# Two transformer layers on one core: products with v in three 16-bit passes, one quad later

## The chip, the cores and the metric

The kernel runs on one core of a Trainium2 chip. A core has five engines that run side by side, each through its own instructions in order: PE (TensorE, matrix products; its weight loads are shown apart as PEld), DVE (VectorE), ACT (ScalarE), POOL (GpSimd) and SP (SyncE, which here issues most DMAs). The metric is the device time of one execution in microseconds (us). A difference under 2% is taken as no change.

## The reference

`x` is 2048 rows of 640 numbers. Two layers follow each other, and both use the same weights; a layer is an attention part and an MLP part. The attention has 32 heads of 20 and a sliding window of 256 rows.

```python
def _A_ref(x, wqkv, wo):
    qkv = (x @ wqkv).reshape(B, S, 3, H, Dh) ...          # H = 32, Dh = 20, S = 2048
    scores = jnp.einsum("bhqd,bhkd->bhqk", q, k) * (Dh ** -0.5)
    mask = (idx[:, None] - idx[None, :] >= 0) & (idx[:, None] - idx[None, :] < 256)
    p = _softmax(jnp.where(mask[None, None], scores, -1e9), axis=-1)
    o = jnp.einsum("bhqk,bhkd->bhqd", p, v)
    return o.transpose(0, 2, 1, 3).reshape(B, S, D) @ wo

def _B_ref(x, w1, b1, w2, b2):
    h = jnp.einsum("bsd,df->bsf", x, w1) + b1             # D = 640, F = 1536
    r = jnp.where(h > 0, h, 0)
    return jnp.einsum("bsf,fd->bsd", r * r, w2) + b2

x = x + _A_ref(_layernorm(x), A_wqkv, A_wo)
x = x + _B_ref(_layernorm(x), B_w1, B_b1, B_w2, B_b2)
...                                                       # the same two lines once more
```

## The kernel before

**Units and quads.** The rows are cut into 8 groups of 256; a unit `u` is one group in one layer, 16 in all (`NU`). In a unit the heads go by fours, 8 quads (`NQ`). A query of a unit sees keys of its own unit and of the unit before (`steps_of`: four key blocks of 128, in three steps; units 0 and 8 see only themselves, in two steps).

**Precision.** The large products (`mm3`, line 327, "dense") take every operand as two f16 numbers, a high one and the rest, and do three passes: high by high, high by rest, rest by high. A rest is made by a pair of operations, ACT writes the high half and DVE subtracts. Only the products with v (`pv_quad`, line 838) run in f32, straight from the exp's output.

**One quad** is this chain, with the names that the trace shows:

- M, `max_quad` (line 653): scores of q and k in the bank pair `bb`. DVE merges (666) and reduces (669) them to row maxima, which go through a transposing DMA into two extra rows of the query tile. M runs three quads ahead of S.
- S, `exp_quad` (line 767): the scores once more, less the maxima, into the same pair `bb`. ACT takes the exp (789) into six f32 buffers `pt`, one for each step and half; POOL zeroes what the mask hides (804, 808).
- V, `pv_quad` (line 838): 16 products of `pt` with `vt`, four heads side by side in 32 columns each, the last row of `vt` giving the row sums. ACT copies the result (850), and SP writes it to DRAM.

Since S and M share `bb`, M(n+3) must wait for the exps of S(n), and S(n+1) for the reductions of M(n+3).

**One unit's dense work**, in `stage_` functions that hand out products a few at a time: q, k and values of unit u+1 (`stage_qk`, `stage_v`), the output product of unit u-1 (`stage_o`, from `od`, which `load_o` fetches from DRAM and divides by the row sums), its layernorm and transposing DMA (`y_cross`), and its MLP (`stage_f`: w1, then relu on ACT, square on POOL and the two halves on ACT and DVE, then w2).

**What sets the order.** The program is written out by a small planner: `now` is its clock for PE, `post` and `pump` put work of the other engines at the time at which the planner thinks that it can start, with costs and priorities given by hand, and `together` deals dense products between S, M and V of a unit. Two banks (`mm_tile`) hold all other results of PE. Each engine then runs its instructions in exactly that order, so a wrong guess becomes a wait.

The core of `together` before:

```python
if kind == "v":
    wants += quad[1][0]
work(part, Want(*wants, bank=kind == "v"))
if kind == "s":
    quad = exp_quad(what[1])
...
if kind == "v":
    pv_quad(what[1], quad)
```

so the order is S, dense, M, V, dense, and V belongs to the S just ahead. In units 14 and 15 some dense work is held back (`CARRY`, `KEEP`) for the end, where the last V's result has to go through DRAM.

## Time and profile before

| what | value |
|---|---|
| median of 2 runs (lowest to highest) | 1580.69 us (1580.55 to 1580.83) |
| the execution that was profiled | 1585.88 us |
| its span, first to last instruction | 1584.2 us |
| busy share of PE, DVE, ACT, POOL | 98%, 59%, 46%, 38% |
| PE without work over the whole span | 29 us |
| of that, before 230 us | 23 us |
| a unit in the middle of a layer | 96.6 us |

The span is read from the page's first line, the idle time of PE from 1584.2 - 1555.0. Durations below come from this one execution; the median of the runs is 3.5 us below its span. A group's line in the profile shows the line of the code, the engine, the operation, what is written and read, the number of instructions, the time in which at least one ran, and the mean of one. The lines on which the argument rests are shown in the prediction.

### The profile page before, as it was taken

What the parts mean: (1) busy time and instruction counts of PE and PEld (TensorE: products, weight loads), DVE (VectorE), ACT (ScalarE), POOL (GpSimd) and SP (SyncE); (2) the same over time, 40 slices, a digit from 0 to 9 for tenths busy, and PEclk for the clock granted to TensorE, in tenths of its full rate; (3) what the DMA queues carried; (4) which work ended last, traced back from release to release, by engine and by line L of the source; (5) the groups of instructions that cost most, each with busy time, mean ns of one, the idle gap of its engine ahead of it and who ended that gap; (6) DMA issues with size and microseconds to landing.
All of it is one profiled execution on the core that took longest, in us unless ns stands there. A gap on an engine that the chain in (4) does not pass through costs nothing.

```text
span 1584.2 us, 51151 instructions
## 1 busy us (share of the span) xinstructions
PE 1555.0 (98%) x21570; PEld 1167.1 (74%) x21570; DVE 928.6 (59%) x1910; ACT 733.5 (46%) x1593; POOL 607.9 (38%) x1291
## 2 busy tenths in 40 slices
PE   8888999999999999999999999999999999999999
PEld 7665778777777777777777777777777777777777
DVE  8776664565655566465465646566465565556542
ACT  4454545345354444534434454444534445445522
POOL 1232535335343352534414253343524435344522
PEclk9999999999999999999999999999999999999999
DMA  9764343352534625345253533525344253441120
GB/s 270 192 175 125 69 116 83 98 115 65 121 80 108 122 50 123 87 106 108 62 138 81 117 91 107 111 54 120 86 120 94 67 132 68 123 90 58 30 65 19
DMA packets 243341, 160.35 MB, mean 101 GB/s; under 512 B 91176, under 2 KB 226856, under 8 KB 243112
## 3 DMA queue, kind: packets, MB, share of 16 engines
q1 hardware_dynamic: 236744, 147.58, 38.6%
q10 hardware_dynamic: 6368, 9.50, 2.0%
q8 instruction: 169, 2.77, 0.8%
q14 instruction: 60, 0.49, 0.1%
HBM read 84.68 MB, written 52.95 MB: 87 GB/s over the span
## 4 chain that ended last, share of the span: by engine, by line
PE 93%; DVE 2%; DMA 2%; ACT 1%; issue 1%; POOL 0%; SPq 0%; ACTq 0%; DVEq 0%; POOLq 0%
PE acc L327 72%; PE pv L838 11%; PE bb L653 5%; PE bb L767 5%; ACT pt L789 1%; DMA x<-in_A_x_dram 1%; PE bb L775 0%; DMA qt<-mT 0%; DVE mx L669 0%; PE bb L678 0%; DVE bb L633 0%; DMA o<-ot 0%; DVE bst L353 0%; DMA xt<-in_A_x_dram 0%; DVE bb L666 0%
## 5 line engine op out<-in xcount | busy, mean ns | idle before, releaser
L789 ACT ACTIVATE pt<-bb 128x512 f32<-128x512 f32 (+1 forms) x736 | 374.0, 600 | 226.0 <-PE bb L767 198.8
L804 POOL TENSOR_SCALAR_AFFINE_SELECT pt<-pt 128x256 f32<-128x256 f32 x448 | 187.2, 420 | 539.7 <-ACT pt L789 525.6
L327 PE MATMUL acc<-y,w_s 128*128 128x256 f16 x2880 | 328.3, 273 | 0.1
L327 PE MATMUL acc<-w_s,hh 128*128 128x320 f16 (+1 forms) x2340 | 326.8, 298 | 0.0
L327 PEld LDWEIGHTS <-w_s 128*128 128x128 f16 x2880 | 276.5, 98 | 51.3 <-issue 15.0
L327 PEld LDWEIGHTS <-hh 128*128 128x128 f16 x2340 | 221.9, 98 | 97.6 <-issue 12.7
L669 DVE TENSOR_REDUCE mx<-bb 128x4 f32<-128x1024 f32 x224 | 273.9, 1223 | 6.6
L327 PEld LDWEIGHTS <-wq_s 128*128 128x128 f16 x2400 | 230.1, 98 | 46.8 <-issue 14.0
L327 PE MATMUL acc<-yT,wq_s 128*128 128x256 f16 x2250 | 258.8, 273 | 2.3 <-DVE qd L510 0.9
L808 POOL TENSOR_SCALAR_AFFINE_SELECT pt<-pt 128x256 f32<-128x256 f32 x512 | 223.1, 458 | 92.3 <-ACT pt L789 91.0
L1023 DVE TENSOR_TENSOR hh<-r,hh 128x256 f16<-128x256 f32 x192 | 94.6, 516 | 225.1 <-ACT hh L1020 218.2
L838 PE MATMUL pv<-pt,vt 128*32 128x128 f32 (+1 forms) x3840 | 189.5, 330 | 0.2 <-POOL pt L804 0.2
L850 ACT COPY ot<-pv 128x256 f32<-128x256 f32 x128 | 47.6, 372 | 286.2 <-PE pv L838 286.2
L1017 POOL TENSOR_TENSOR r<-r 128x256 f32<-128x256 f32 x192 | 114.2, 616 | 157.9 <-ACT r L1013 155.9
L666 DVE COPY_PREDICATED bb<-maskq,bb 128x256 f32<-128x256 uint16 x224 | 93.3, 423 | 98.6 <-PE bb L653 96.8
L327 PE MATMUL acc<-wo_s,od 128*128 128x320 f16 x960 | 140.5, 302 | 3.4 <-DVE od L924 1.9
L838 PEld LDWEIGHTS pv<-pt,vt 128*32 128x32 f32 x3840 | 104.8, 109 | 40.1 <-POOL pt L808 5.5
L327 PE MATMUL acc<-wq_s,yT 128*128 128x320 f16 x900 | 130.6, 300 | 1.4 <-DVE y L378 0.9
L327 PEld LDWEIGHTS <-od 128*128 128x128 f16 x960 | 91.8, 98 | 48.6 <-issue 6.4
L1013 ACT ACTIVATE r<-acc,b1s 128x256 f32<-128x256 f32 x192 | 80.5, 471 | 85.8 <-PE acc L327 84.7
L327 PEld LDWEIGHTS <-yT 128*128 128x128 f16 x900 | 85.5, 98 | 40.7 <-issue 7.8
L364 POOL TENSOR_TENSOR bmv<-bmv,neghalf 128x1 f32<-128x1 f32 x64 | 45.2, 712 | 156.0 <-DVE bmv L358 155.5
(96 smaller groups left out, 1241.6 us busy)
## 6 DMA issues: line engine op xcount, KB each, us to landing
qt<-qk SPq DMA_DIRECT2D x30, 480.0 KB
kt<-qk SPq DMA_DIRECT2D x30, 480.0 KB
qk<-qd SPq DMA_DIRECT2D x17, 640.0 KB
o<-ot SPq DMA_DIRECT2D x256, 42.0 KB
od<-o SPq DMA_DIRECT2D x14, 640.0 KB
qk<-yl SPq DMA_DIRECT2D x13, 640.0 KB
qk<-qd SPq DMA_DIRECT2D x17, 320.0 KB
xt<-in_A_x_dram SPq DMA_DIRECT2D x16, 320.0 KB
```

The source lines that it names most:

```text
L327: nc.tensor.matmul(acc, lhs(a, c), rhs(b, c), start=(k == 0), stop=(k == 3 * nk - 1))
L653: nc.tensor.matmul(flat[e][rows, o:o + b - a], qt[r, p, i * P + 64 * h:i * P + 64 * (h + 1)], kt[r, p, a + to:b + to], start=True, stop=Tr ...
L666: nc.vector.copy_predicated(wins[:, :, 4 * Q:], later, wins[:, :, :Q])
L669: nc.vector.tensor_reduce(most, wins[:, :, Q:], axis=mybir.AxisListType.X, op=ALU.max)
L767: nc.tensor.matmul(bb[e][rows, k, o + a:o + b], kt[r, 2 * qd + j, ko + 64 * h:ko + 64 * (h + 1)], qt[r, 2 * qd + j, q0 * P + a:q0 * P + b] ...
L789: nc.scalar.activation(box["pt"][:, :o], bb[e][:, k, :o], AF.Exp, scale=SCALE / (QS * QS))
L804: nc.gpsimd.affine_select(out=m, in_=m, pattern=[[0, 2], [-1, P]], compare_op=ALU.is_gt, fill=0.0, base=0, channel_multiplier=1)
L808: nc.gpsimd.affine_select(out=m, in_=m, pattern=[[0, 2], [1, P]], compare_op=ALU.is_ge, fill=0.0, base=0, channel_multiplier=-1)
L838: nc.tensor.matmul(pv[32 * jj:32 * (jj + 1), q0 * P:(q0 + qn) * P], vf[:, c:c + 32], pj[:, j, :], start=(k == 0), stop=(k == len(steps) - ...
L1013: nc.scalar.activation(box["r"], acc[:, f, :], AF.Relu, bias=b1s[:, f0 + f:f0 + f + 1], scale=1.0 / (YS * WS))
L1017: nc.gpsimd.tensor_tensor(box["r"], box["r"], box["r"], op=ALU.mult)
L1023: nc.vector.tensor_sub(hh[:, 1, f, :], box["r"], hh[:, 0, f, :])
```

## The change

It does four things.

1. From unit 2 on (`WHOLE = 2`), the values are stored as two f16 halves in the same bytes, and a probability is read as two 16-bit numbers out of one f32 word: its upper 16 bits as bf16 (`hi`), and an f16 rest that is written over its lower 16 bits (`lo`). The products with v run three passes: hi by high, lo by high, hi by rest. The exp gets a bias (`lift`, a factor of 2^10). The rests are new subtractions (`low` in `exp_quad`): per quad of three steps six of 512 columns, four on DVE and two on POOL (all on DVE in the last six quads). `stage_v` gets a subtraction on DVE too. A product of f32 was two records in the profile; a product of 16 bits is one, with a weight load of its own.
2. `pv_quad` of a quad no longer follows its own S: it is held in `behind` and put right after the S of the next quad (`beside`), or after an M where the planner finds it ready.
3. `load_o` is cut in two: `fetch_o` starts the load from DRAM as soon as the last `pv_quad` of a unit is put, into a ring `r` that the MLP uses for its relu (five buffers in place of four), and `load_o` does the division.
4. `stage_v` is no longer at a fixed place among the dense work: a new `Pair` hands out its products when the other dense work has to wait.

Some priorities change (0.8 and 0.9 in place of 1 or 2), and `flow` waits for all masks of a quad in place of the first step's.

```diff
+WHOLE = 2
...
+    def values(u, i):
+        raw = vts[(2 * u + i) % 6]
+        if u < WHOLE:
+            vf = raw.unsqueeze(1)
+        else:
+            vf = raw.bitcast(F16).rearrange("p (a n) -> p a n", a=2)
+        return vf, vf[:, :, :H * (DH + 1)].rearrange("p a (h d) -> p a h d", d=DH + 1)
...
+    class Pair:
...
+        def go(self):
+            c = None if self.mid else self.first.go()
+            if c is None:
+                c = self.fill.go()
+                self.mid = c is not None
+                if c is None:
+                    c = self.first.go()
+            return c
...
 def stage_v(u, which=range(4)):
+        if u > 2:
+            yield Want(unread[u - 2], bank=False)
...
+                def low(hd=hd, src=src):
+                    nc.vector.scalar_tensor_tensor(hd[:, 1], src, s, hd[:, 0], op0=ALU.mult, op1=ALU.subtract)
...
-    def exp_quad(n):
+    def exp_quad(n, beside=None):
...
+        if beside is not None:
+            pv_quad(*beside)
...
-                    nc.scalar.activation(box["pt"][:, :o], bb[e][:, k, :o], AF.Exp, scale=SCALE / (QS * QS))
+                    halves = box["pt"].rearrange("p (n a) -> p n a", a=1)
+                    box["lo"] = halves.bitcast(F16)[:, :, 0]
+                    box["hi"] = halves.bitcast(BF16)[:, :, 1]
+                    nc.scalar.activation(box["pt"][:, :o], bb[e][:, k, :o], AF.Exp, bias=lift, scale=SCALE / (QS * QS))
...
+                    on, eng, each = nc.vector, "D", 1.1
+                    if 2 * k + e in (3, 5) and n < NQ * NU - 6:
+                        on, eng, each = nc.gpsimd, "G", 1.95
+
+                    def low(a=a, b=b, box=box, on=on):
+                        on.tensor_tensor(box["lo"][:, a:b], box["pt"][:, a:b], box["hi"][:, a:b], op=ALU.subtract)
...
+                passes = (("hi", 0), ("lo", 0), ("hi", 1)) if uv >= WHOLE else (("pt", 0),)
+                for m, (b, a) in enumerate(passes):
...
+                                nc.tensor.matmul(pv[32 * jj:32 * (jj + 1), q0 * P:(q0 + qn) * P],
+                                                 vf[:, a, c:c + 32], pj[:, j, :], start=(k == 0 and m == 0),
+                                                 stop=(k == len(steps) - 1 and m == len(passes) - 1),
+                                                 skip_group_check=True, tile_position=(0, 32 * jj))
...
+        if qd == NQ - 1:
+            unread[u].end = now[0]
+            fetch_o(u, u >= NU - 2)
...
+    def fetch_o(u, late=False):
+
+        need(*hjs.pop(u - 1, ()))
...
+            val = sb.tile([P, KC, T], F32, name="ov", tag="r", bufs=1)
...
             if kind == "s":
-                quad = exp_quad(what[1])
+                behind.append((what[1], exp_quad(what[1], behind.pop() if values else None)))
...
-            parts += [stage_qk(u + 1, (0,)), stage_v(u + 1, range(2)), stage_o(u - 1), lambda: (y_cross(u - 1), iter(()))[1], stage_qk(u + 1, (1,)), stage_v(u + 1, range(2, 4))]
+            parts += [stage_qk(u + 1, (0,)), stage_o(u - 1), lambda: (y_cross(u - 1), iter(()))[1], stage_qk(u + 1, (1,))]
+            fill = stage_v(u + 1)
```

**How PE's order changes.** Counted from the two instruction orders, with the number of dense products between the groups (qkv is `stage_qk` and `stage_v`, o is `stage_o`). Before, units 3 to 13 are all alike; now each unit differs, and units 4 to 7 come again as 10 to 13 with small changes. A `|` stands ahead of each S.

```
units 3 to 13 before:
| S qkv50 M V qkv25 | S qkv30 o15 M V o30 | S o15 qkv25 M V qkv40 | S qkv37 M V qkv3 w1 35
| S w1 45 M V w1 35 | S w1 45 M V w1 20 w2 16 | S w2 36 M V w2 28 | S w2 36 M V w2 28
unit 2 now:
| S qkv45 M V qkv82 | S qkv3 o27 M o33 qkv50 | S V qkv25 M w1 15 | S V w1 30 M w1 45
| S V w1 25 M w1 45 | S V w1 20 w2 4 M w2 32 | S V w2 20 M w2 36 | S V w2 24 M w2 4 V w2 24
unit 10 now:
| S V qkv30 M qkv38 | S V qkv22 o15 M o45 qkv75 | S V w1 15 M w1 35 | S V w1 35 M w1 45
| S V w1 35 M w1 15 w2 20 | S V w2 24 M w2 28 | S V w2 24 M w2 32 | S V w2 16 M qkv25
unit 11 now:
| S V qkv35 M qkv45 | S V qkv30 M o60 qkv50 | S V qkv25 M w1 20 | S V w1 35 M w1 45
| S V w1 35 M w1 40 | S V w1 5 w2 24 M w2 36 | S V w2 24 M w2 32 | S V w2 24 M w2 4 qkv10
unit 12 now:
| S V qkv40 M qkv40 | S V qkv30 M qkv15 o42 | S V o18 qkv5 M qkv70 | S V w1 30 M w1 40
| S V w1 35 M w1 40 | S V w1 35 M w2 44 | S V w2 24 M w2 32 | S V w2 24 M w2 12 V w2 8 qkv5
unit 13 now:
| S qkv45 M qkv85 o15 | S V o23 M o22 qkv75 | S V M w1 40 | S V w1 35 M w1 45
| S V w1 30 M w1 30 w2 8 | S V w2 24 M w2 32 | S V w2 24 M w2 32 | S V w2 24 M qkv45
unit 15 and the end, before:
| S w2 24 M V w2 16 | S w2 28 M V w2 4 o23 | S o22 M V o15 w2 4 | S w2 24 M V w2 8 tr8
| S tr2 w1 25 M V w1 20 | S w1 40 V w1 25 | S w1 40 V | S w1 30 V w2 108 o60 w2 16 tr5 w2 12 tr5 w2 8 w1 180 w2 180
unit 15 and the end, now (unit 14 ends with M V):
| S M o45 | S V o15 tr5 M tr5 w1 25 | S V w1 35 M w1 60 | S V w1 30 M w1 30 w2 20
| S V w2 24 M w2 40 | S V w2 40 V | S w2 20 V | S V o60 tr10 w1 180 w2 180
```

Three of these places word for word. The end on PE; `vt` are values, `hh` with `w_s` is w2 of unit 14, `od` with `wo_s` the output product of unit 15. Before:

```order
L838 MATMUL pv<-pt,vt_93 32x256 x4
L838 MATMUL pv<-pt,vt_92 32x128 x4
L838 MATMUL pv<-pt,vt_89 32x128 x4
L838 MATMUL pv<-pt,vt_88 32x256 x4
L327 LDWEIGHTS hh
L327 MATMUL acc<-w_s,hh 128x320
```

and now:

```order
L912 LDWEIGHTS vt_90
L912 MATMUL pv<-pt,vt_90 32x256
L912 LDWEIGHTS vt_90
L912 MATMUL pv<-pt,vt_90 32x256
L363 LDWEIGHTS od
L363 MATMUL acc<-wo_s,od 128x320
```

The 108 products of w2 that stood between the last V and the output product have moved ahead of it.

Unit 13, third quad, on PE, ahead of M (L653 before, L706 now; `kt` and `qt` are keys and queries). Before, products of `stage_qk` stand there:

```order
L327 MATMUL acc<-yT,wq_s 128x256
L327 LDWEIGHTS wq_s
L327 MATMUL acc<-yT,wq_s 128x256
L653 LDWEIGHTS qt
L653 MATMUL bb_133<-kt_85,qt 64x256
```

and now V of the second quad:

```order
L912 LDWEIGHTS vt_92
L912 MATMUL pv<-pt,vt_92 32x256
L706 LDWEIGHTS qt
L706 MATMUL bb_135<-kt_87,qt 64x256
L706 LDWEIGHTS qt
L706 MATMUL bb_136<-kt_87,qt 64x256
```

V has moved from behind M to between S and M, and 25 products of q, k or values have moved ahead of S.

On DVE, around the merge (COPY_PREDICATED) and the reduction of M while w1 goes over to w2; `hh` is the MLP's rest. Before:

```order
L1023 TENSOR_TENSOR hh<-r,hh 128x256 x6
L666 COPY_PREDICATED bb_133<-maskq,bb_133 128x4x64
L669 TENSOR_REDUCE mx<-bb_133 128x4
L666 COPY_PREDICATED bb_134<-maskq,bb_134 128x4x64
L669 TENSOR_REDUCE mx<-bb_134 128x4
L1023 TENSOR_TENSOR hh<-r,hh 128x256 x2
```

and now (in a quad of unit 8, whose own key block has 256 columns):

```order
L1112 TENSOR_TENSOR hh<-r,hh 128x256 x2
L880 TENSOR_TENSOR pt<-pt 128x512 x2
L880 TENSOR_TENSOR pt<-pt 128x256
L1112 TENSOR_TENSOR hh<-r,hh 128x256 x2
L719 COPY_PREDICATED bb_135<-maskq,bb_135 128x4x64
L722 TENSOR_REDUCE mx<-bb_135 128x4
L719 COPY_PREDICATED bb_136<-maskq,bb_136 128x4x64
L722 TENSOR_REDUCE mx<-bb_136 128x4
L1112 TENSOR_TENSOR hh<-r,hh 128x256 x2
```

The subtractions `pt<-pt` have come between the MLP's work and the merge.

More of the change, by code (lines that the diff above doesn't have):

```diff
@@ L1112, in portion, with together @@
             yield c
-    def together(ns, ms, dense, cost, share=1.0, whole=True, after=None, pace=0):
+    def together(ns, ms, dense, cost, share=1.0, whole=True, after=None, pace=0, flush=False, fill=()):
         ts = list(turns(ns, ms, pace))
@@ L1118, in together @@
         done = part = 0.0
-        quad = None
-        s = Stream(dense)
+        s = Pair(dense, iter(fill))
         def work(part, w):
@@ L1144, in together @@
                 wants += [trips[m // NQ, j, m % NQ] for j in range(2)]
-            if kind == "v":
-                wants += quad[1][0]
-            work(part, Want(*wants, bank=kind == "v"))
+            values = kind == "s" and bool(behind)
+            if values:
+                wants += [j for ms in behind[0][1][1] for j in ms]
+            if kind is None and m is None and behind:
+                work(part, Want(*(j for ms in behind[0][1][1] for j in ms)))
+                pv_quad(*behind.pop())
+            work(part, Want(*wants, bank=values))
             if kind == "s":
-                quad = exp_quad(what[1])
+                behind.append((what[1], exp_quad(what[1], behind.pop() if values else None)))
                 for it in late:
@@ L1270 @@
         share = 1.0 - KEEP / cost if last else 1.0 - CARRY / cost if u == NU - 2 else 1.0
-        together(quads, ahead, dense, cost, share, u < NU - 2, after=(lambda: load_o(u - 1, last)) if u > 1 else None, pace=NQ)
+        if last:
+            load_o(u - 1, True)
+        together(quads, ahead, dense, cost, share, u < NU - 2, after=(lambda: load_o(u - 1)) if 1 < u < NU - 1 else None, pace=NQ, flush=u >= NU - 2, fill=fill)
     load_o(NU - 1, True)
```

175 lines of the change are left out of this document (110 added, 65 removed).

## The prediction

> **What bounds the kernel now.** I read the page first, then busy time by stretches, then one quad (four heads of one unit) in order of time, then the end. The page:
>
> ```profile
> span 1584.2 us, 51151 instructions
> PE 1555.0 (98%) x21570; PEld 1167.1 (74%) x21570; DVE 928.6 (59%) x1910; ACT 733.5 (46%) x1593; POOL 607.9 (38%) x1291
> PE 93%; DVE 2%; DMA 2%; ACT 1%; issue 1%; POOL 0%; SPq 0%; ACTq 0%; DVEq 0%; POOLq 0%
> ```
>
> PE is the chain. By stretches (span, then PE, PEld, DVE, ACT and POOL busy with counts, granted clock, DMA share, GB/s):
>
> ```profile
> 124.00:136.00 12.00, 7.33 (x65) 4.15 (x63) 5.58 (x14) 4.40 (x8) 3.58 (x9) 0.72 0.59 158
> 230.00:1380.00 1150.00, 1149.99 (x16376) 865.28 (x16366) 671.44 (x1321) 532.52 (x1160) 456.09 (x976) 1.00 0.42 98
> 1380.00:1512.00 132.00, 128.88 (x2030) 95.55 (x2033) 71.43 (x134) 71.44 (x159) 67.53 (x146) 1.00 0.25 61
> 1512.00:1584.00 72.00, 69.15 (x598) 54.55 (x586) 23.44 (x53) 14.62 (x36) 13.42 (x21) 1.00 0.15 46
> ```
>
> From 230 to 1380 us PE does not stop once: 1149.99 of 1150. So there the time is PE's work, every us taken off it is a us gained, and any new wait of PE is a us lost in full. One quad there, by order of time (start, duration):
>
> ```profile
> 1046.75 0.75 PE L767 MATMUL bb<-qt,kt 62*64 62x192 f16 x32
> 1047.44 5.06 PE L327 MATMUL acc<-w_s,hh 128*128 128x320 f16 x36
> 1047.55 3.05 ACT L789 ACTIVATE pt<-bb 128x512 f32<-128x512 f32 x6 [0.68 <-PE bb L767]
> ...
> 1050.32 1.12 POOL L808 TENSOR_SCALAR_AFFINE_SELECT pt<-pt 128x256 f32<-128x256 f32 x3
> ...
> 1052.43 0.76 PE L653 MATMUL bb<-kt,qt 60*64 60x256 f16 x38
> ...
> 1053.12 1.51 PE L838 MATMUL pv<-pt,vt 128*32 128x256 f32 x32
> 1053.30 0.43 DVE L666 COPY_PREDICATED bb<-maskq,bb 128x256 f32<-128x256 uint16 x1
> ...
> 1054.56 3.98 PE L327 MATMUL acc<-w_s,hh 128*128 128x320 f16 x28
> ...
> 1055.36 1.23 DVE L669 TENSOR_REDUCE mx<-bb 128x4 f32<-128x1024 f32 x1
> ...
> 1058.46 0.75 PE L767 MATMUL bb<-qt,kt 62*64 62x192 f16 x32
> ```
>
> I call L767 S (scores), L653 M (row maxima of a later quad), L838 V (products with v), L327 dense. S and M share the bank pair bb, so each waits for the other's reader: M for the exps of S, which end 3.85 us after S starts (1047.55 + 3.05 - 1046.75); S for the reductions of M, which end 4.16 us after M starts (1055.36 + 1.23 - 1052.43). Here M comes 5.68 us after S and S 6.03 us after M: 1.8 and 1.9 us to spare. That spare time is why PE never waits.
>
> **The change, part by part.**
>
> *V in halves.* V takes 1054.56 - 1053.12 = 1.44 us. Dense takes (1052.43 - 1047.44) / 36 = 0.139 us for 320 columns, 0.433 ns a column. A quad's V is 16 products, two blocks of 256 and two of 128 columns for four heads that run side by side: 768 columns a pass. f32 as four passes is 4 x 0.333 = 1.33, which leaves 0.11 us to fill and drain. Three f16 passes: 1.00 + 0.11 = 1.11 us, 0.33 less. Units 3 to 7 and 9 to 15 have 96 such quads; unit 8 has eight of half the work and unit 2 eight with half the blocks in halves: 104 quads' worth, **-34 us**. Bounds: the passes at exactly 3/4 of 1.44 give -37. On the other side stand the weight loads, now 48 a quad instead of 32:
>
> ```profile
> 1004.27 1.03 PEld L838 LDWEIGHTS pv<-pt,vt 128*32 128x32 f32 x32
> ```
>
> At their 0.032 us each they would need 1.54 us: +10. S and M issue 32 and 38 f16 products in 0.69 us (1047.44 - 1046.75, 1053.12 - 1052.43), 0.018 to 0.022 us each, and 48 of those need 0.87 to 1.04 us, so I take -34. The Trainium skill ("TensorE: Matmul & The Clock Gate", section "Wait — 56ns, not 53.3ns?") says that starts never come closer than about 25 ns; by it V would be 48 x 25 ns + 0.11 = 1.31 us and the gain an estimated 14 us. M's 38 in 0.69 us disagree with it.
>
> *V behind S.* The exps write six buffers, and V of the quad before, which reads them, now stands right behind S. The first exp therefore waits for V's first third as well, about 0.37 us: M's earliest place becomes S + 4.2. S's stays M + 4.2.
>
> *The order of PE.* The front part lists the dense products between the groups. Short places, with 0.113 us for a product of 256 columns and 0.139 for one of 320: unit 2 has M to S with 15 products of 256, 2.3 of 4.2 us needed (-1.9). In the same way: unit 4, 0.75; unit 5, 2.3 in three places; unit 6, 1.9; unit 7, 2.9, most of it where V stands directly before M (1.8 of 4.2 us); unit 10, 0.75; unit 11, 2.3; unit 12, 1.9; unit 13, 2.4; unit 14, 0.75; unit 15, 6.0 (S comes after M and V alone, and then M follows S with nothing between). Sum **+24 us**, where the row of 230 to 1380 had 0.01. The dense products that stood there are not lost: they ran earlier, where od or y2 was waited for, values first.
>
> *The end.* Today's rows:
>
> ```profile
> 1507.21 0.75 PE L767 MATMUL bb<-qt,kt 62*64 62x192 f16 x32
> ...
> 1507.89 3.45 PE L327 MATMUL acc<-y,w_s 128*128 128x256 f16 x30
> ...
> 1511.01 1.12 POOL L808 TENSOR_SCALAR_AFFINE_SELECT pt<-pt 128x256 f32<-128x256 f32 x3
> 1511.27 1.55 PE L838 MATMUL pv<-pt,vt 128*32 128x256 f32 x32
> ...
> 1512.75 14.84 PE L327 MATMUL acc<-w_s,hh 128*128 128x320 f16 x108
> ...
> 1527.43 8.31 PE L327 MATMUL acc<-wo_s,od 128*128 128x320 f16 x60
> ...
> 1535.58 2.34 PE L327 MATMUL acc<-w_s,hh 128*128 128x320 f16 x16
> ...
> 1541.57 6.62 PE L327 MATMUL acc<-y,w_s 128*128 128x256 f16 x58
> ```
>
> The last V's way through DRAM to od (1512.75 to 1527.43, 14.7 us) lies under 108 products of unit 14; the layernorm (1535.58 to 1541.57, 6.0 us) under 36 more. In the new order V is followed at once by the 60 of od, and these by the transposes: unit 14's products are all gone. So PE waits some 13 us there (14.7, less what the adds of those products held DVE up) and 4.7 before w1. The last S has no dense product before its V: the last mask ends 4.92 us after S (1511.01 + 1.12 - 1507.21), the last subtraction (0.66, below) at 5.6, and V would be due at 1.8: 4.2 with its last passes; the quad before, with 20 products, 1.4. Sum **+23 us**; the bounds are 12 (od ready sooner) and 28.
>
> *Clock.* The longest wait of PE today costs more than itself:
>
> ```profile
> PE tr L731 <- DVE x L949: 3.4, 1, 3.4
> ```
>
> Behind it the clock granted over 124 to 136 us is 0.72, which is 3.4 us of 12. Waits of 13 and 4 us at the end, and those of unit 15, may each bring one to three of these: **+5** (0 to 9). Today's own waits after 1380 (3.1 of 132, a part at the same layernorm and od) go: **-2**.
>
> *The new subtractions.* Per full quad six of 512 columns, four on DVE and two on POOL, and four on DVE for a unit's values. The nearest rows:
>
> ```profile
> L1023 DVE TENSOR_TENSOR hh<-r,hh x192: 361/426/860, 159.7 to 1563.7; 128x256 f16<-128x256 f32 x192
> L444 DVE TENSOR_TENSOR yl<-xt,yl x52: 814/817/834, 190.8 to 1399.5; 128x640 f16<-128x640 f32 x52
> L1017 POOL TENSOR_TENSOR r<-r x192: 605/612/1149, 158.5 to 1562.7; 128x256 f32<-128x256 f32 x192
> ```
>
> Between 256 and 640 columns DVE's 512 come to 0.66 us (361 to 817 ns); the order has 420: +277 us, plus 56 for the values at about 0.43: DVE goes from 928.6 to some 1230 us, 77%. POOL's 188 at twice 612 ns add 230: 838 us, 53%. Both stand off PE's path as long as the spare 1.8 us hold, and by the lists above only some 0.8 are left. L1023 shows 361 ns at best and 860 at worst, L1017 605 and 1149: the two engines hold each other up when both read SBUF. For delays of PE from this I take **+12 us**, one for each unit with halves; bounds 0 and 65 (second rival).
>
> *Nothing:* the exp's bias, values at another scale, value rows in the ring (off PE, and the waits for od are counted above).
>
> **Sum.** 1584.2 - 34 + 24 + 23 + 5 - 2 + 12 = 1612 us of span. The execution profiled took 1585.88; the median of the runs, 1580.69, is 3.5 us below its span. I take off 4 to 5: **1607 us, +1.7%**.
>
> **Rivals.**
> 1. *The waits are covered* (faster). M may start before the last exp, and a later quad may catch up. Price: without the 24, 23, 5 and 12, 1584.2 - 36 - 3.5 = 1545 us; with half of them 1577. Against it: no product stands in those places. It decides if PE's busy share stays at 98%.
> 2. *DVE and POOL become the bound* (slower). In the w1 stretch a quad has 11.2 us (5.6 + 5.6 in the new order). If SBUF reads of the two exclude each other, 8 masks at 0.37, 5.3 squares (80 dense products, 15 to each) at 0.61 and 2 subtractions at 1.22 on POOL make 8.6, four at 0.66 and 5.3 at 0.36 on DVE 4.5: 13.1. At three such quads in 12 units that is up to 65 us in place of 12: 1660; with half, 1635. It decides from about 0.5 us a quad. For it: the pairs of ends above. Against: the rows hold some start-up that need not exclude. The Trainium skill ("SBUF — State Buffer", section "Who interferes with whom") states this as a rule: a VectorE operation with two inputs in SBUF and a GpSimd one that reads SBUF lock each other out for the whole instruction.
> 3. *The halves do not run at pace* (no gain in V). If weights or operands four bytes apart slow the passes to today's 1.44 us: 1607 + 34 = 1641.
>
> **Chances.** Forecast 0.42 (1585 to 1612), rival 1 0.17 (0.07 of it below 1549), rival 2 0.33, rival 3 0.08. Two per cent, about what a measurement of this kernel can tell from no change, are 1549 and 1612 us. Faster 0.07; within 0.42 + 0.10 = 0.52; slower 0.33 + 0.08 = 0.41. The range leaves out the lower half of rival 1 and the far end of rival 2: 1576 to 1645; the forecast's own is 1585 to 1612.
>
> **What would show it.** V: groups of 1.1 us on PE. Order: waits of PE on ACT's pt and DVE's mx of 1 to 3 us, once a unit, and none before. End: one PE gap of over 10 us in front of the od products, and a granted clock below 1 behind it. Subtractions: DVE near 77%, POOL near 53%, and POOL's masks longer than 406 ns where rival 2 holds. I am wrong if PE's idle time stays under 40 us (rival 1) or if waits on DVE and POOL sum to more than 60 (rival 2).

## The result, and the profile after

The changed kernel takes 1762.57 us (median of 2 runs, 1761.62 to 1763.53) against 1580.69: the ratio is 1.115, with a 95% interval from 1.110 to 1.120. It is 182 us slower. The profiled execution took 1761.62 us, its span is 1759.9.

From the page of the changed kernel: the span, the busy times, and the shares of the chain that ended last.

```profile
span 1759.9 us, 55219 instructions
...
PE 1591.2 (90%) x23234; PEld 1203.9 (68%) x23234; DVE 1323.7 (75%) x2417; ACT 799.5 (45%) x1593; POOL 954.2 (54%) x1495
...
PE 33%; DVE 24%; POOL 15%; ACT 13%; issue 11%; DMA 3%; SPq 1%; POOLq 0%; ACTq 0%; DVEq 0%
```

V's products (count, busy us, mean ns), before and after:

```profile
L838 PE MATMUL pv<-pt,vt 128*32 128x128 f32 (+1 forms) x3840 | 189.5, 330 | 0.2 <-POOL pt L804 0.2
L912 PE MATMUL pv<-pt,vt 128*32 128x128 bf16 (+5 forms) x5504 | 164.0, 261 | 12.4 <-DVE pt L880 4.0
```

PE is idle for 168.7 us (1759.9 - 1591.2) where it was idle for 29.2, and it is busy for 36 us longer, although V's own busy time fell by 25.5. PE was 93% of the chain; now DVE, POOL and ACT together have more of it than PE. No engine but PE is above 75%, so this isn't an engine that ran out of time.

The waits of PE in the changed kernel (sum, times, longest, in us):

```profile
PE bb L820 <- DVE mx L722: 66.3, 76, 1.8
PE bb L706 <- ACT pt L848: 24.9, 44, 3.1
PE acc L363 <- ACT od L1007: 18.2, 3, 10.5
PE tr L784 <- DVE x L1035: 6.0, 1, 6.0
```

L820 is S, L706 is M, L363 dense, and L912 V. S waits for the reductions of M (L722), and M for the exps of S (L848): both waits are on the bank pair `bb`. The stretches that the prediction looked at, and the end (span, then PE, PEld, DVE, ACT and POOL busy with counts, granted clock, DMA share, GB/s):

```profile
230.00:1380.00 1150.00, 1065.74 (x16119) 811.38 (x16117) 907.36 (x1588) 528.48 (x1054) 692.97 (x1057) 0.99 0.37 89
1570.00:1690.00 120.00, 85.28 (x1332) 60.17 (x1330) 80.85 (x125) 47.74 (x96) 59.99 (x96) 0.87 0.11 33
1690.00:1760.00 70.00, 55.09 (x430) 42.45 (x430) 20.40 (x47) 13.18 (x32) 12.15 (x18) 0.86 0.11 36
```

In the first, PE was idle for 0.01 us before and is for 84 now. One quad there, in order of time (start, duration, in brackets the idle time ahead of it and what ended that):

```profile
1088.61 0.27 PE L820 MATMUL bb<-qt,kt 62*64 62x192 f16 x1
...
1089.25 0.75 PE L820 MATMUL bb<-qt,kt 62*64 62x192 f16 x31 [0.38 <-DVE mx L722]
...
1089.93 1.23 PE L912 MATMUL pv<-pt,vt 128*32 128x256 bf16 x48
...
1090.56 0.69 ACT L848 ACTIVATE pt<-bb,lift 128x512 f32<-128x512 f32 x1 [1.09 <-PE pv L912]
...
1091.09 4.00 PE L363 MATMUL acc<-y,w_s 128*128 128x256 f16 x35
...
1093.37 1.87 ACT L848 ACTIVATE pt<-bb,lift 128x512 f32<-128x512 f32 x3
1093.42 1.15 DVE L880 TENSOR_TENSOR pt<-pt 128x512 f16<-128x512 f32 x1 [0.26 <-POOL pt L863]
...
1095.02 1.03 PE L706 MATMUL bb<-kt,qt 60*64 60x256 f16 x38
...
1095.76 0.92 DVE L880 TENSOR_TENSOR pt<-pt 128x512 f16<-128x512 f32 x1 [1.19 <-POOL pt L867]
...
1095.97 5.08 PE L363 MATMUL acc<-y,w_s 128*128 128x256 f16 x45
1096.04 1.78 POOL L867 TENSOR_SCALAR_AFFINE_SELECT pt<-pt 128x256 f32<-128x256 f32 x3
1096.59 0.61 DVE L1112 TENSOR_TENSOR hh<-r,hh 128x256 f16<-128x256 f32 x1
...
1097.49 0.91 DVE L880 TENSOR_TENSOR pt<-pt 128x512 f16<-128x512 f32 x1 [0.30 <-POOL pt L867]
1097.79 1.48 POOL L880 TENSOR_TENSOR pt<-pt 128x512 f16<-128x512 f32 x1
1098.30 1.25 DVE L1112 TENSOR_TENSOR hh<-r,hh 128x256 f16<-128x256 f32 x1
...
1099.47 0.41 DVE L719 COPY_PREDICATED bb<-maskq,bb 128x256 f32<-128x256 uint16 x1
...
1101.20 0.24 PE L820 MATMUL bb<-qt,kt 62*64 62x192 f16 x1
...
1101.52 1.22 DVE L722 TENSOR_REDUCE mx<-bb 128x4 f32<-128x1024 f32 x1
...
1102.79 0.75 PE L820 MATMUL bb<-qt,kt 62*64 62x192 f16 x31 [1.35 <-DVE mx L722]
```

Read it as a loop. The exps of S end at 1095.24, 6.6 us after the first product of S (before: 3.85). That product is alone: it uses the first bank of the pair, and the other 31 wait until the maxima of the second bank are reduced. M starts at 1095.02, but DVE touches its result only at 1099.47. Four operations stand ahead in DVE's queue: two subtractions, which wait for POOL's masks (1.19 and 0.30 us), and two rests of the MLP (L1112). The second of these takes 1.25 us, beside a subtraction on POOL; over the whole run L1112 has a median of 0.42 us with nothing on POOL beside it and of 0.63 with something. The last reduction ends at 1102.74, 7.7 us after M (before: 4.16), and the rest of the next S has waited for it for 1.35 us. V itself does what was predicted: 48 products in 1.16 us (1089.93 to 1091.09).

The end, rows of the same kernel:

```profile
1686.23 0.62 PE L912 MATMUL pv<-pt,vt 128*32 128x256 f16 x7 [0.23 <-DVE pt L880]
...
1694.18 0.96 DVE L1000 RECIPROCAL rs<-rs 128x64 f32<-128x64 f32 x2 [8.00 <-DMA rs<-o]
...
1697.40 11.33 PE L363 MATMUL acc<-wo_s,od 128*128 128x320 f16 x60 [10.55 <-ACT od L1007]
...
1712.62 0.76 PE L427 MATMUL bb<-ident,xt 128*128 128x128 f32 x5 [3.35 <-DVE xt L402]
```

The last V's way through DRAM leaves PE idle for 10.55 us, and the 60 products behind it take 11.33 us in place of 8.31; the granted clock of the stretch is 0.86.

### The profile page after: what moved, and what is told of

Read it like the earlier page. It is cut to its first block, busy times and chain, and to the rows that moved or that the text cites. A ratio compares the mean times of both kernels' runs of the same rounds, so it can differ in the third digit from the quotient of the medians.

```text
span 1759.9 us, 55219 instructions
## 1 busy us (share of the span) xinstructions
PE 1591.2 (90%) x23234; PEld 1203.9 (68%) x23234; DVE 1323.7 (75%) x2417; ACT 799.5 (45%) x1593; POOL 954.2 (54%) x1495
## 3 DMA queue, kind: packets, MB, share of 16 engines
q1 hardware_dynamic: 236744, 147.58, 33.5%
## 4 chain that ended last, share of the span: by engine, by line
PE 33%; DVE 24%; POOL 15%; ACT 13%; issue 11%; DMA 3%; SPq 1%; POOLq 0%; ACTq 0%; DVEq 0%
PE acc L363 23%; ACT pt L848 10%; DVE mx L722 7%; POOL pt L867 6%; DVE pt L880 5%; PE pv L912 4%; POOL pt L863 4%; PE bb L820 3%; DVE hh L1112 2%; POOL pt L880 2%; DVE bb L719 2%; POOL r L1106 1%; PE bb L706 1%; POOL bmv L400 1%; ACT r L1102 1%
## 5 line engine op out<-in xcount | busy, mean ns | idle before, releaser
L848 ACT ACTIVATE pt<-bb,lift 128x512 f32<-128x512 f32 x736 | 450.8, 691 | 293.8 <-PE pv L912 241.5
L880 DVE TENSOR_TENSOR pt<-pt 128x512 f16<-128x512 f32 (+1 forms) x436 | 378.5, 879 | 237.6 <-POOL pt L863 141.1
L863 POOL TENSOR_SCALAR_AFFINE_SELECT pt<-pt 128x256 f32<-128x256 f32 x448 | 225.0, 505 | 488.6 <-ACT pt L848 458.8
L363 PE MATMUL acc<-y,w_s 128*128 128x256 f16 x2880 | 340.3, 278 | 2.2 <-DVE y L414 1.2
L363 PE MATMUL acc<-w_s,hh 128*128 128x320 f16 (+1 forms) x2340 | 331.4, 298 | 3.7 <-DVE hh L1112 3.7
L363 PEld LDWEIGHTS <-w_s 128*128 128x128 f16 x2880 | 280.6, 100 | 54.1 <-issue 13.0
L867 POOL TENSOR_SCALAR_AFFINE_SELECT pt<-pt 128x256 f32<-128x256 f32 x512 | 272.6, 554 | 78.4 <-ACT pt L848 78.4
L363 PEld LDWEIGHTS <-hh 128*128 128x128 f16 x2340 | 221.2, 98 | 99.7 <-issue 9.9
L722 DVE TENSOR_REDUCE mx<-bb 128x4 f32<-128x1024 f32 x224 | 272.2, 1221 | 5.2
L363 PE MATMUL acc<-yT,wq_s 128*128 128x256 f16 x2250 | 258.3, 273 | 4.9 <-DVE yl L546 1.5
L363 PEld LDWEIGHTS <-wq_s 128*128 128x128 f16 x2400 | 230.9, 98 | 42.4 <-issue 9.3
L880 POOL TENSOR_TENSOR pt<-pt 128x512 f16<-128x512 f32 (+1 forms) x204 | 247.8, 1232 | 1.3
L912 PE MATMUL pv<-pt,vt 128*32 128x128 bf16 (+5 forms) x5504 | 164.0, 261 | 12.4 <-DVE pt L880 4.0
L1112 DVE TENSOR_TENSOR hh<-r,hh 128x256 f16<-128x256 f32 x192 | 124.2, 674 | 52.3 <-ACT hh L1109 50.3
L820 PE MATMUL bb<-qt,kt 62*64 62x64 f16 (+3 forms) x3552 | 101.1, 234 | 68.9 <-DVE mx L722 66.3
L363 PE MATMUL acc<-wo_s,od 128*128 128x320 f16 x960 | 143.1, 307 | 21.3 <-ACT od L1007 18.2
L1106 POOL TENSOR_TENSOR r<-r 128x256 f32<-128x256 f32 x192 | 131.6, 705 | 34.9 <-ACT r L1102 34.6
L820 PEld LDWEIGHTS <-kt 62*64 62x64 f16 x3552 | 70.2, 108 | 103.8 <-issue 98.1
L363 PEld LDWEIGHTS <-od 128*128 128x128 f16 x960 | 94.0, 100 | 66.2 <-ACT od L1007 19.4
L706 PE MATMUL bb<-kt,qt 60*64 60x64 f16 (+3 forms) x4256 | 107.4, 224 | 25.7 <-ACT pt L848 24.9
L363 PE MATMUL acc<-wq_s,yT 128*128 128x320 f16 x900 | 128.2, 299 | 0.5 <-DVE kt L414 0.5
```

The lines of the kernel that those rows point to most:

```text
L363: nc.tensor.matmul(acc, lhs(a, c), rhs(b, c), start=(k == 0), stop=(k == 3 * nk - 1))
L706: nc.tensor.matmul(flat[e][rows, o:o + b - a], qt[r, p, i * P + 64 * h:i * P + 64 * (h + 1)], kt[r, p, a + to:b + to], start=True, stop=Tr ...
L722: nc.vector.tensor_reduce(most, wins[:, :, Q:], axis=mybir.AxisListType.X, op=ALU.max)
L820: nc.tensor.matmul(bb[e][rows, k, o + a:o + b], kt[r, 2 * qd + j, ko + 64 * h:ko + 64 * (h + 1)], qt[r, 2 * qd + j, q0 * P + a:q0 * P + b] ...
L848: nc.scalar.activation(box["pt"][:, :o], bb[e][:, k, :o], AF.Exp, bias=lift, scale=SCALE / (QS * QS))
L863: nc.gpsimd.affine_select(out=m, in_=m, pattern=[[0, 2], [-1, P]], compare_op=ALU.is_gt, fill=0.0, base=0, channel_multiplier=1)
```

## The experiments

All are single executions with a profile; the kernel before, run beside them, took 1581.2 to 1582.1 us. The planner decides PE's order anew whenever a product, a dependency or a price that it knows of changes. In runs 1, 3 and 8 to 11 it wrote PE's order of the changed kernel, product for product. In runs 2, 5, 6, 7 and 12 to 15 it wrote another, so these compare the order too; run 4 starts from the kernel before. "A" in the first expectations is the theory that the subtractions cost the time, "B" that the order does.

**1. No subtractions.**

```diff
 def low(a=a, b=b, box=box, on=on):
-    on.tensor_tensor(box["lo"][:, a:b], box["pt"][:, a:b], box["hi"][:, a:b], op=ALU.subtract)
+    pass
...
-pj = box[b][:, part]
+pj = box["hi" if b == "lo" else b][:, part]
```

> The changed kernel with every instruction in its order but the 640 subtractions that make the rests of the probabilities (436 on DVE, 204 on POOL): they are left out, and the pass that would read a rest reads the upper half again. Theory A (the subtractions, by the time they take and by blocking on DVE and POOL, push the reductions, exps and masks back, and PE waits for those): most of the 182 us go, 1595 to 1640 us. Theory B (the order itself, V between S and the exps and the short places between the groups, makes the waits): 1700 us or more.

Measured 1642.4, just above the range of theory A: the subtractions of the probabilities cost 120 us, and some 60 are left. PE's order is the same, and DVE's too but for the subtractions.

**2. Values whole**, the rest of the change kept: `WHOLE = 16` in place of 2.

> All values and probabilities stay whole (f32 products with v, no subtractions), and the rest of the change stays: V one quad later, value rows in the ring, values filling waits; the order is planned anew for it. Theory A: 1580 to 1610 us. Theory B: 1650 us or more, since V still stands between S and the exps.

Measured 1644.2: 62 us of loss in a kernel without any halves. It is not run 1 with whole values, though. With f32 products the planner puts V right behind M in 83 of the 128 quads and right behind S in 42; in the changed kernel it is 21 and 102. That the two times agree doesn't show what V's passes are worth.

**3. Exp without bias.** `bias=lift` taken out of the exp, everything else as changed.

> The changed kernel with the exp's bias left out (the factor 2^10 on the probabilities is missing, nothing else differs). In the changed kernel one exp takes 696 ns at the median against 605 before. If the bias makes that, exps return to about 605 ns and, with six of them in each quad's chain, the time falls by 30 to 60 us; if the exp is longer for another reason (the four-byte words it writes are read by others at the time), both stay.

Measured 1747.5, 15 us less, half of the least that was expected. Run 4 takes the bias by itself; runs 1 and 8, and 2 and 5, differ by it alone.

**4. The kernel before, with a bias in its exp.**

```diff
-nc.scalar.activation(box["pt"][:, :o], bb[e][:, k, :o], AF.Exp, scale=SCALE / (QS * QS))
+nc.scalar.activation(box["pt"][:, :o], bb[e][:, k, :o], AF.Exp, bias=lift, scale=SCALE / (QS * QS))
```

> The kernel before, with a bias operand (zero) in the exp and nothing else. The prediction priced the bias at nothing. If its 90 ns an exp fit into the 1.8 us that M has to spare: 1580 to 1587. If they do not: 1595 or more, with waits of PE on ACT's pt.

Measured 1597.3, 16 us more. The groups of the exp (count, busy, mean ns), first of the kernel before, then of this one:

```profile
L789 ACT ACTIVATE pt<-bb 128x512 f32<-128x512 f32 (+1 forms) x736 | 374.0, 600 | 226.0 <-PE bb L767 198.8
```

```profile
L791 ACT ACTIVATE pt<-bb,lift 128x512 f32<-128x512 f32 (+1 forms) x736 | 440.6, 687 | 222.4 <-PE bb L769 193.2
```

One operand that is read from SBUF makes each exp 87 ns longer. The stretch from 230 to 1380 us of this kernel shows that it reaches PE without a wait to be seen:

```profile
230.00:1380.00 1150.00, 1149.72 (x16257) 860.77 (x16254) 663.38 (x1309) 573.62 (x1152) 446.00 (x970) 1.00 0.40 97
```

PE is as busy as before at the same clock, but gets through 16257 products in place of 16376. Over the whole run it is idle for 29.0 us, as before (29.2), and busy for 1566.6 us in place of 1555.0 with the same products. Stalls too short to be counted as idle would do that; that they are what the profile counts as busy is argued, not shown. The Trainium skill ("ScalarE: Activation LUTs", section "What ACT_TABLE_LOAD costs") says that an operand of one number per partition adds about 93 ns to an ACTIVATE; the traces agree with their 87.

**5. Values whole and no bias** (runs 2 and 3 together).

> Values whole, no subtractions, no bias, V one quad later: the order alone. The kernel with the bias took 1644. If the order makes those 62 us: 1630 to 1640. If the exps, 90 ns longer each by the bias, make them: 1585 to 1610.

Measured 1612.5: the order that the planner writes for whole values, that of run 2, costs 31 us, and the bias on top of it 32 (1644.2). From the first S of the last unit to the end of the span it takes 153.7 us (1457.1 to 1610.8), where the kernel before took 139.7 (1444.5 to 1584.2). That is 14 of the 31; a unit in mid-run takes 97.3 in place of 96.6, and unit 14 takes 7 more.

**6. V at its own quad**, with the halves, the subtractions and the bias.

```diff
-yield 1 - share, None, m
+yield 1 - share, ("v", n), m
...
-behind.append((what[1], exp_quad(what[1], behind.pop() if values else None)))
+quad = exp_quad(what[1])
...
+if kind == "v":
+    pv_quad(what[1], quad)
```

> The changed kernel with V back at its own quad: M, then V of the quad whose scores were just taken, as before the change. Halves, subtractions, the bias, the filling and the ring stay. Theory 1 (V one quad later is the dear part of the order: standing right behind S it delays every exp and so every M): most of the 60 us that were left without subtractions come back, 1690 to 1725. Theory 2 (the delay is what hides the subtractions; without it PE waits for them ahead of every V): 1780 or more, with waits of PE on DVE's and POOL's pt above 60 us.

Measured 1928.8. The first theory fell: with V at its own quad PE waits for the subtractions ahead of every V, so the shift by a quad is needed. The waits of PE in this kernel:

```profile
PE pv L912 <- POOL pt L880: 161.7, 149, 3.9
PE pv L912 <- DVE pt L880: 57.6, 39, 4.0
```

**7. V at its own quad, values whole, no bias**: what is left is the filling, the ring and the new priorities.

> V at its own quad, values whole in every unit (no halves, no subtractions) and no bias in the exp: what is left of the change is the filling with the values projection, the ring that takes the value rows, and new priorities. Theory 1 (V's place and the bias): 1575 to 1592, as before the change. Rival (the filling and the early fetch leave od and the layernorm with nothing beside them): 1610 or more.

Measured 1631.9, so the rest of the change costs by itself, 50 us in this order. Part is one wait: at the end of unit 8 PE stands still for 9.8 us until the maxima's transposing DMA has landed,

```profile
PE bb L820 <- DMA qt<-mt: 11.7, 6, 9.8
```

and units 8 to 10 take 100, 101 and 99 us in place of 88, 97 and 97; unit 1 takes 110 in place of 101. Which of the three parts makes the planner write that order was not tried.

**8. Halves without subtractions or bias** (runs 1 and 3 together).

> The changed kernel without the subtractions of the probabilities (the second pass reads the upper halves again) and without the bias in the exp. Values whole and no bias took 1612.5, so this shows the halves alone. If V's 25 us less of PE work come off the end: 1580 to 1598. If the shorter quads only make PE wait sooner for the exps and maxima: 1605 to 1620, as with the bias, where 1644 and 1642 were the same.

Measured 1619.0, in PE's order of the changed kernel; run 1 adds only the bias to it, 23 us. V's products are busy for 33.5 us less than in the kernel before (189.5):

```profile
L912 PE MATMUL pv<-pt,vt 128*32 128x128 bf16 (+3 forms) x5504 | 156.0, 257 | 2.1 <-POOL pt L863 1.9
```

PE is idle for 76 us (1617.3 - 1541.3), 47 more than before; from 230 to 1380 us it is 23.4, where the kernel before had 0.01. With values whole it was 1612.5, but in another order, so the 6 us between the two are not the worth of the halves.

**9. An operation with one input in place of DVE's subtraction** (half of the probability, not the rest).

```diff
+if on is nc.vector:
+    nc.vector.tensor_scalar(box["lo"][:, a:b], box["pt"][:, a:b], 0.5, None, op0=ALU.mult)
+else:
     on.tensor_tensor(box["lo"][:, a:b], box["pt"][:, a:b], box["hi"][:, a:b], op=ALU.subtract)
```

> The changed kernel with DVE's subtraction replaced by an operation of the same size, input and output that reads one operand in SBUF and not two (half of the probability in place of its rest); POOL's stay. If the two engines' SBUF reads block each other (theory A, by blocking), DVE's operation falls from 911 ns to 600 to 680 at the median, POOL's masks return to about 410 ns, and the time falls by 40 to 110 us. If it is DVE's load alone, the time stays within 20 us of 1762.

Measured 1687.6. But the operation is also shorter (451 ns at the tenth percentile, the subtraction 728), so this run alone doesn't separate blocking (two engines that hold each other up) from load. Nor is it free of blocking: its median is 456 ns with nothing on POOL beside it and 637 with something. Those of the subtraction in the changed kernel are 723 and 917.

**10. Two such operations of 256 columns**, to give DVE its load back.

> DVE's subtraction of a 512-column block is two one-input operations of 256 columns (half of the probability each, in place of the rest); POOL's subtractions stay. One operation of 512 with one input took 451 ns at best and gave 1688; the subtraction takes 711 at best and gave 1762. Two of 256 take about 600. If the 75 us are blocking between DVE and POOL (two inputs against one): 1685 to 1705. If they are DVE's time alone: 1725 to 1755.

Measured 1729.0, with DVE busy for 1324.4 us, as in the changed kernel (1323.7), and POOL for 833 in place of 954. So 41 of the 75 us are DVE's time, and 34 come with POOL's instructions being held up less (its masks of L867 fall from 554 to 461 ns on average, its subtractions from 1232 to 1060). The split is rough: these operations may meet POOL's in other ways.

**11. POOL's subtractions left out.** For POOL's blocks `box["lo"] = box["hi"]`.

> POOL's 204 subtractions are left out (their second pass reads the upper halves again); DVE's 436 stay as they are. If POOL's subtractions hold up masks and DVE as much as their share of the work (204 of 640): 1715 to 1730. If they are the heavier part, being 1.2 us each and in the same queue as the masks: 1700 or less. If they stand in idle time of POOL: 1750 or more.

Measured 1720.8: 204 of the 640 subtractions cost 42 of the 120 us, about their share.

**12. The planner with measured prices.**

```diff
-ex = post("A", 50 + 0.834 * o, power, ...
+ex = post("A", 140 + 1.08 * o, power, ...
-ms.append(post("G", 375, mask, ex, ...
+ms.append(post("G", 530, mask, ex, ...
-on, eng, each = nc.vector, "D", 1.1
+on, eng, each = nc.vector, "D", 1.6
-    on, eng, each = nc.gpsimd, "G", 1.95
+    on, eng, each = nc.gpsimd, "G", 2.3
...
```

> The whole change, with the planner's prices set to the durations that its own trace shows: exp 140 + 1.08 a column (693 ns for 512), masks 530, subtractions 60 + 1.6 a column on DVE and 60 + 2.3 on POOL, squares 705, their rests 674. M then stands later behind S with more products between, and the last two quads of a unit have none. If the loss is an order written with too short prices: 1700 to 1735. If it is the work itself, which the order can only move about: 1750 to 1790, the waits now at the two quads without products.

Measured 1862.3, worse than either expectation. M goes further behind S, the dense products of a unit are used up early, and its last two quads have none: S, V, M, S, V, M. What that does, in order of time:

```profile
536.55 0.27 PE L820 MATMUL bb<-qt,kt 62*64 62x192 f16 x1
539.40 0.75 PE L820 MATMUL bb<-qt,kt 62*64 62x192 f16 x31 [2.58 <-DVE mx L722]
540.08 2.10 PE L912 MATMUL pv<-pt,vt 128*32 128x256 bf16 x48
...
545.00 0.37 PE L706 MATMUL bb<-kt,qt 60*64 60x256 f16 x1 [2.82 <-ACT pt L848]
545.58 1.28 PE L706 MATMUL bb<-kt,qt 60*64 60x256 f16 x37 [0.21 <-ACT pt L848]
549.35 0.31 PE L820 MATMUL bb<-qt,kt 62*64 62x192 f16 x1 [2.50 <-DVE mx L722]
```

and the stretch around it:

```profile
536.00:554.00 18.00, 8.88 (x203) 6.12 (x202) 9.85 (x16) 4.78 (x9) 7.48 (x12) 0.62 0.14 41
```

The same V takes 2.10 us here in place of 1.23; the granted clock of the stretch is 0.62. Better prices don't help where the work to fill the waits isn't there.

**13. Subtract first, then mask.** The two halves share one 32-bit word, so a mask that comes after the subtraction zeroes both; DVE then waits for the exp alone. All work stays, and the planner writes PE's and DVE's order anew (V right behind S in 97 quads, 102 in the changed kernel).

```diff
-ms.append(post("G", 375, mask, ex, ...))
+ms.append(mask)
...
-ms = [post(eng, 60 + each * (b - a), low, *ms, ...)]
+low_ = post(eng, 60 + each * (b - a), low, ex, ...)
-ls.extend(ms)
+ls.extend(post("G", 375, m, low_, ...) for m in ms)
```

> The whole change with each subtraction ahead of its block's masks: it waits for the exp alone, and the mask then zeroes the word that holds both halves. All work stays. If DVE's queue, standing still behind POOL's masks with the reductions of M behind it, is what lengthens the loop over bb: M to its last reduction falls from a median of 7.2 to about 5.5 us and the time to 1680 to 1715. If it is the load or the blocking: 1745 or more, since both stay (POOL's queue then waits for DVE instead).

Measured 1679.3, 83 us less with not one instruction of work taken out. How much of it the new order makes by itself was not tried. The subtractions of DVE (count, busy, mean ns, then the idle time ahead of them and what ended it), in the changed kernel and in this one:

```profile
L880 DVE TENSOR_TENSOR pt<-pt 128x512 f16<-128x512 f32 (+1 forms) x436 | 378.5, 879 | 237.6 <-POOL pt L863 141.1
```

```profile
L881 DVE TENSOR_TENSOR pt<-pt 128x512 f16<-128x512 f32 (+1 forms) x436 | 341.8, 824 | 160.9 <-ACT pt L848 155.8
```

and PE's wait for the maxima, 66.3 us in the changed kernel, here:

```profile
PE bb L820 <- DVE mx L722: 27.3, 36, 2.0
```

What DVE does between the first product of M and its last reduction says more (mean of the quads of units 3 to 7 and 9 to 13). In the changed kernel this stretch is 7.5 us, of which subtractions take 1.71 and waits for POOL's masks 0.37. In run 1 it is 6.1 with neither. In run 13 it is 6.4, with 0.60 of subtractions and no wait for masks: most of the subtractions now lie outside it.

**14 and 15. The same without bias, and the same with all subtractions on DVE.**

> The same without the bias in the exp. 90 ns less in each of six exps of a quad; the bias was worth 15 us with subtractions behind masks and 23 to 32 without subtractions. Expected 15 to 30 below the kernel with the bias; if the loop over bb is no longer the bound, 10 or less.

> As the first of these, with all subtractions on DVE and none on POOL. POOL's 204 were worth 42 us in the changed kernel; DVE gets 204 more at 0.7 to 0.9 us. If POOL's share is the dearer: 15 to 40 below the first. If DVE's load is the bound (it would be near 80% busy): 20 or more above it.

Measured 1663.9 (15 less) and 1740.4 (61 more). With 640 subtractions in DVE's queue, where the reductions of M stand too, DVE is busy for 1395.7 us (80%), and PE's wait for the maxima is back at 65.9. The best of the variants with halves and subtractions, 1663.9, is still 83 us slower than the kernel before; none tried here beats it.

**The loop over bb in all of them.** For the quads of units 3 to 7 and 9 to 13 (unit 8 has two steps in place of three) the table gives medians in us: the time from the first product of S to the end of the last exp that reads it, and from the first product of M to the end of its last reduction. The last column is the share of these M whose reductions are still running when the next S starts. A quad of the kernel before lasts 12.07 us (a unit's 96.6 by 8).

| kernel | time | S to exps | M to reductions | sum | S starts before M is reduced |
|---|---|---|---|---|---|
| before | 1581 | 4.11 | 4.16 | 8.3 | 0% |
| 4, before with bias | 1597 | 4.56 | 4.17 | 8.7 | 0% |
| 5, values whole, no bias | 1613 | 4.30 | 4.50 | 8.8 | 14% |
| 8, halves, no subtractions, no bias | 1619 | 4.83 | 4.85 | 9.7 | 12% |
| 1, no subtractions | 1642 | 5.28 | 4.96 | 10.2 | 15% |
| 2, values whole | 1644 | 4.75 | 4.70 | 9.5 | 22% |
| 14, subtract first, no bias | 1664 | 5.01 | 5.72 | 10.7 | 38% |
| 13, subtract first | 1679 | 5.58 | 5.65 | 11.2 | 38% |
| 9, one input | 1688 | 6.00 | 6.14 | 12.1 | 49% |
| 11, POOL's subtractions out | 1721 | 6.10 | 6.40 | 12.5 | 61% |
| 10, one input, twice | 1729 | 6.08 | 6.81 | 12.9 | 61% |
| 15, all on DVE | 1740 | 6.38 | 6.28 | 12.7 | 49% |
| 3, changed, no bias | 1748 | 5.93 | 6.65 | 12.6 | 68% |
| changed | 1763 | 6.30 | 6.71 | 13.0 | 68% |

In each bank S cannot start again before M's reductions, nor M before S's exps. Since the first product needs the first bank alone, the two stretches can overlap (by 1.5 us in the quad shown), so their sum is a measure of the loop and not a strict lower bound. Before, the sum was 3.8 us shorter than a quad, and no S started with reductions still running. In the changed kernel it is 13.0 of the 13.4 us that a quad then lasts, and two of three S do. Runs 6, 7 and 12 aren't in the table: in 6 PE waits for V's operands, in 7 the loop is as short as before (8.2), and in 12 the products run out.

## Why the prediction was wrong

Run 8, run 1 and the changed kernel have one and the same order on PE, and along them the 182 us come apart: 38 for the order, V's halves and the rest of the change together (1580.7 to 1619.0), 23 for the bias (1642.4), 120 for the subtractions. In the prediction's own terms, the sum without its 12 for the subtractions is a span of 1600; run 8's is 1617.3. So of the 148 us by which the span was missed, some 107 are the subtractions, 23 the bias, and 17 all the rest.

- **The subtractions (+12, bounds 0 and 65): the step that failed; they cost 120.** The prediction counted DVE's and POOL's time and asked whether it fits. It does: 75% and 54%. What it left out is the place in DVE's queue. It said "S's stays M + 4.2", as if M's reductions kept their place; in fact they stand behind subtractions that stand behind masks, and M's reductions end 6.71 us after M. The new order on DVE, with the subtractions ahead of the merge, was there to be read ahead of the prediction, and it wasn't followed through. Run 1 shows the cost in an unchanged order on PE. For the mechanism, run 13 turns subtraction and mask round and gains 83 of the 120 us with the same work; its order on PE changed too, so the 83 may not be this alone, but the subtractions inside M's stretch fall from 1.71 to 0.60 us and the wait for masks there from 0.37 to nothing. What is left (37 us) fits the load and POOL's longer instructions of runs 10 and 11, but wasn't taken apart in that kernel. Two counts were off as well, with little effect: the order has 436 subtractions on DVE and 204 on POOL, not 420 and 188, and DVE's terms add up to 1262 us, not 1230.
- **V in halves (-34): right on PE.** A V took 1.16 us where 1.11 was forecast, the weight loads didn't hold it up, and in run 8 V's busy time is 33.5 us less. What that is worth in time, "every us taken off it is a us gained", isn't shown: runs 1 and 2, and 8 and 5, differ by -2 and +6 us, but between different orders.
- **The second rival** had the right engines and a wrong mechanism: it priced full blocking as lack of capacity in three quads of a unit, 65 us (half of it makes 1628, not 1635). POOL's instructions did get longer (the masks of L867 from 458 to 554 ns), and run 10 puts about 34 us on that. Its test, waits on DVE and POOL above 60 us, was met by the first row of the waits alone.
- **The bias (nothing): wrong.** It cost 16 us in the kernel before (run 4), 32 with values whole (runs 5 and 2), 23 in the changed order without subtractions (runs 8 and 1) and 15 with them (run 3). It was put down as free without a row for its duration. It lies in the loop: 87 ns on each of six exps of a quad.
- **V behind S (M's earliest place from 3.85 to 4.2): undersized.** In run 8 the median from S to its first exp goes from 0.84 to 1.30 us, 0.46 where 0.37 was forecast. In the changed kernel it is 2.0, since the first product of S now often runs ahead of a wait for the second bank's maxima (0.38 and 1.35 us in the quad shown), and V and the exps come after that. Run 6 shows that the shift is needed all the same.
- **Short places and the end (+24 and +23): right without the subtractions.** Run 8 has this order, and PE's idle time there is 47 us above the kernel before: 23.4 us from 230 to 1380 where it had 0.01, and the last unit with the end is 23 us longer (162.4 us against 139.7). In the changed kernel the end is 43 us longer (1578 to 1760), since the last quads also wait for subtractions and masks. The one gap of over 10 us before od is there as forecast; the waits on ACT's pt and DVE's mx, forecast once a unit, number 120 (44 and 76).
- **The clock (+5, 0 to 9): undersized.** The mean granted clock went from 0.997 to 0.975. The trace's record of the clock has it at one half for 89 us of the changed kernel, and PE was busy in 60 of them, so its products lost at most 30 us by it, against at most 4 before. In run 8 it is at most 15. These are part of the sums above. The prediction looked for long waits only; see below.
- **Rival 1** (waits covered) and **rival 3** (halves not at pace) did not happen.

The slower side had 0.41; the forecast of 1607 stood on spare time that its own steps had already cut to 0.8 us a quad, and the range ended at 1645, about the time of run 1, which has no subtraction of probabilities at all.

## What to carry to other kernels

Where two users share a buffer in turns, add up the whole round (each product, its readers, and all that stands ahead of these readers in their queues) and hold the sum against the work between; busy shares say nothing of it. An instruction that waits for another engine holds up everything behind it in its queue, so make it depend on the earliest thing that it can (here: subtract before the mask, 83 us together with the order that the planner then wrote). When a planner writes the order anew for a variant, the variant compares two orders as well: runs that keep the order are those that can be put in one sum. And before an operand is called free, look for a row of the same operation with and without it.

## What the runs showed of the hardware

- Waits of less than 3 us can be enough for the clock to fall. In run 12 PE is busy without a break from 524 to 536 us, then waits 2.58 us, and the record of the granted clock goes to one half at 540.1. None of the waits from 536 to 554 us is longer than 2.82 us, PE is busy for 8.88 of these 18 us, and the granted clock there is 0.62. Over the whole run it is 0.917; it is at one half for 307 us, and PE was busy in 192 of them, so at most 96 us were lost by it. The Trainium skill ("TensorE: Matmul & The Clock Gate", section "HAM oscillation — how this bites in real kernels") gives the rule that gaps must not exceed about 3.4 us. These are shorter, and the measurement decides. The Trainium skill ("TensorE: Matmul & The Clock Gate", section "A second HAM failure mode: psum-queue depth-cycling") tells of short and frequent idling that makes the clock swing; with that the trace agrees.
- 48 products of 256 and 128 columns in three 16-bit passes take 1.16 us, and their starts lie 20 ns apart (median of the groups without a wait inside; 14 to 16 ns for M's 38). The Trainium skill ("TensorE: Matmul & The Clock Gate", section "Wait — 56ns, not 53.3ns?"), which the prediction weighed, has starts never closer than about 25 ns; by that V would take an estimated 1.31 us. The measurement decides.
- Two engines' operations lengthen when they run beside each other. DVE's subtraction in the changed kernel has a median of 723 ns with nothing on POOL beside it and of 917 with something, and the one-input operation of run 9 of 456 and 637.
- With a bias in the exp PE is "busy" for 1149.7 of 1150 us, as without, and gets through 0.7% fewer products (run 4). The count of instructions in a stretch shows it, the busy share doesn't.
